# Causal attention with beacon keys and a SwiGLU FFN on one core: a scheduler-ordered kernel rewritten as one pipeline in fixed order

## The chip, the core and the metric

One core of a Trainium2 chip. TensorE (PE) multiplies, VectorE (DVE) and ScalarE (ACT) read its results from PSUM, GpSimd (POOL) works on SBUF alone, SyncE (SP) issues DMAs. PSUM has eight banks of 2 KB a partition. The metric is the device time of one execution in microseconds; lower is better.

## The reference

Eight batches, eight heads, 576 queries of 64 values. Every query sees 16 beacon keys and, causally, the 576 keys of its own batch and head. The head outputs are put side by side into 4,608 tokens of 512 values, and a gated FFN of width 1,536 follows.

```python
k_all = np.concatenate([beacon_k, k], axis=2)          # 16 + 576 keys
v_all = np.concatenate([beacon_v, v], axis=2)
scores = np.matmul(q, k_all.transpose(0, 1, 3, 2)) / np.sqrt(64)
scores = np.where(causal, -1e9, scores)                # beacons are never masked
a = np.exp(scores - scores.max(-1, keepdims=True))
a /= a.sum(-1, keepdims=True) + 1e-09
x = np.matmul(a, v_all).transpose(0, 2, 1, 3).reshape(4608, 512)
g = x @ w_gate                                         # 512 x 1536
out = (g / (1 + np.exp(-g)) * (x @ w_val)) @ w_out     # 1536 x 512
```

## The kernel before

**Inputs.** `batch_inputs` loads a batch of q, k and v with 17 DMAs from SP's queue, rows of 256 bytes (one head, one token), all heads at once into float32 staging tiles with one buffer each, and casts them to bf16 on VectorE (L102 to L110). Beacons and keys stand together in five key tiles of 128, 128, 128, 128 and 80 rows; the queries are in blocks of 128 from the first query on, the last of 64 rows. The three weights are loaded and cast by three large DMAs from GpSimd's queue, issued at the start (L119 to L123).

**Attention.** `pair_transposes` turns q and k of two heads (one head in the upper, one in the lower 64 rows) with five PE transposes each (L239, L249), and VectorE copies them out (L245, L255). `head` then goes over five key tiles: a score matmul over 64 rows, keys on the output partitions (L280, L283, L297), an Exp to bf16 on ScalarE (L285, L286, L299), on GpSimd a memset (L302) and a causal select (L287, L304). P·V (L335) takes P as the weights and V with a column of ones as the 65 moving columns, so each output has its own row sum; VectorE divides (L354 to L362) and writes to `x_all`, whose rows are tokens in blocks of 128 over all batches. As 576 is not a multiple of 128, odd batches begin half a block later, and 17 matmuls a head are needed.

**FFN.** `ffn_chunk_stages` cuts a chunk of 512 tokens into 45 pieces of work: the transposes of x (L139, L145); for each of 12 slices of the width the gate (L159) and value matmuls (L169), four each, and the elementwise step; for each of four token tiles two halves of six output matmuls (L206, L217), a copy (L224) and a DMA from GpSimd's queue (L226). The elementwise step needs Tanh and a Copy on ScalarE and two operations on VectorE:

```python
nc.scalar.activation(th[:, 0:L], g_ps[:, 0:L], ACT.Tanh, scale=0.5)   # L180
nc.scalar.activation(vv[:, 0:L], v_ps[:, 0:L], ACT.Copy, scale=0.5)   # L182
nc.vector.scalar_tensor_tensor(                                       # L184
    out=u[:, 0:L], in0=th[:, 0:L], scalar=1.0, in1=g_ps[:, 0:L],
    op0=ALU.add, op1=ALU.mult,
)
```

**Order.** Chunks whose tokens the batches before have finished go into a list; `gap()` takes one piece of it after each key tile and each query block of a head. What is left, two chunks of nine, runs after the last batch. The framework's scheduler may then move instructions on each engine by its own priorities. PSUM: four one-bank buffers for transposes, scores and outputs, three for gate and value, one for P·V.

## Time and profile before

| | |
|---|---|
| three timed runs | 545.87, 546.08 and 548.62 us, median 546.08 |
| span of the profiled execution, first to last instruction | 541.7 us |
| PE, DVE, ACT, POOL busy | 86, 49, 46 and 28% of the span |
| first PE instruction | 31.1 us |
| attention of the second batch begins | 70 us |
| granted TensorE clock, mean | 0.977 of 2.4 GHz |

The page gives busy time as the union of an engine's instructions. TensorE's matmuls overlap in the pipe, so the distance from one start to the next tells its pace, not the duration. An idle time counts only where the engine is the bottleneck. The profiled execution's time is its span and what lies around it; the runs above were timed without the profiler.

### The profile page before, as it was taken

The page shows a single profiled execution, that of the slowest core. Times are in us where ns is not written, and L with a number is a line of the kernel's source. Part 1 is how long each engine was busy: PE and PEld are TensorE (multiplying, and loading weights), DVE is VectorE, ACT ScalarE, POOL GpSimd, SP SyncE. Part 2 cuts the span into 40 slices and gives each one's busy share as a digit, 9 for nine tenths or more (in the row PEclk, how much of TensorE's full clock was granted, in tenths as well). Part 3 has the DMA queues.
Part 4 walks back from the last instruction along what each step waited for, and adds up shares of the span by engine and source line. Part 5 has one row for each costly group of instructions (what it writes and reads, how often), then busy time and mean ns, then how long its engine had stood idle before and what let it go on. Part 6 is the DMA issues. An engine that isn't in the chain of part 4 may idle for free.

```text
span 541.7 us, 9489 instructions
## 1 busy us (share of the span) xinstructions
PE 463.3 (86%) x3177; PEld 220.2 (41%) x3232; DVE 267.6 (49%) x656; ACT 249.9 (46%) x601; POOL 151.0 (28%) x629
## 2 busy tenths in 40 slices
PE   0028989988999799898999799879999998999995
PEld 0015544434454444443444344434444444444442
DVE  0033358645656446635554465545443554364552
ACT  0004536722674256624762377225752675263460
POOL 3005424323334222342324223322333232200001
PEclk9999999989999989998999799979999999999999
DMA  9999545456523630094008500010002000201102
GB/s 170 202 225 252 122 91 123 106 131 168 122 59 74 188 85 1 7 238 102 1 2 203 142 2 2 27 52 1 1 1 79 1 1 2 79 0 40 39 2 77
DMA packets 120353, 43.61 MB, mean 81 GB/s; under 512 B 115440, under 2 KB 116976, under 8 KB 120304
## 3 DMA queue, kind: packets, MB, share of 16 engines
q1 hardware_dynamic: 114816, 28.84, 24.0%
q0 software_dynamic: 5488, 14.16, 9.3%
q8 instruction: 25, 0.41, 0.3%
q14 instruction: 24, 0.20, 0.1%
HBM read 38.27 MB, written 9.44 MB: 88 GB/s over the span
## 4 chain that ended last, share of the span: by engine, by line
PE 68%; issue 15%; SPq 6%; DVE 6%; ACT 2%; POOL 2%; DMA 1%; POOLq 0%; DVEq 0%; ACTq 0%
PE g_ps L159 14%; PE v_ps L169 14%; PE s_ps L297 8%; PE o_ps L335 8%; PE o_ps L206 7%; PE o_ps L217 7%; PE s_ps0a L280 4%; SPq L74 3%; SPq L91 2%; PE xt_ps L139 2%; PE qt_ps L239 2%; PE kt_ps L249 1%; DVE kt_pair L255 1%; DVE v5p L109 1%; ACT pT L299 1%
## 5 line engine op out<-in xcount | busy, mean ns | idle before, releaser
L299 ACT ACTIVATE pT<-s_ps 128x464 bf16<-128x464 f32 (+3 forms) x256 | 91.0, 402 | 58.7 <-PE s_ps L297 55.4
L159 PE MATMUL g_ps<-xT,wg 128*128 128x512 bf16 x404 | 113.2, 388 | 3.7 <-DVE xT L145 1.8
L184 DVE SCALAR_TENSOR_TENSOR u<-th,g_ps 128x512 bf16<-128x512 bf16 x108 | 74.2, 687 | 82.5 <-ACT th L180 81.3
L169 PE MATMUL v_ps<-xT,wv 128*128 128x512 bf16 x421 | 112.9, 381 | 1.0 <-ACT vv L182 0.3
L285 ACT ACTIVATE pT<-s_ps0a 128x512 bf16<-128x512 f32 x64 | 38.2, 596 | 129.4 <-PE s_ps0b L283 125.5
L304 POOL TENSOR_SCALAR_AFFINE_SELECT pT<-pT 128x128 bf16<-128x128 bf16 (+1 forms) x256 | 72.8, 295 | 87.3 <-ACT pT L299 85.4
L180 ACT ACTIVATE th<-g_ps 128x512 bf16<-128x512 f32 x108 | 64.9, 601 | 55.9 <-PE g_ps L159 55.9
L287 POOL TENSOR_SCALAR_AFFINE_SELECT pT<-pT 128x112 bf16<-128x112 bf16 x64 | 24.8, 388 | 214.0 <-ACT pT L285 203.7
L182 ACT ACTIVATE vv<-v_ps 128x512 bf16<-128x512 f32 x108 | 64.7, 599 | 31.5 <-PE v_ps L169 31.2
L335 PEld LDWEIGHTS <-pT 128*128 128x128 bf16 (+3 forms) x1088 | 52.8, 104 | 34.6 <-issue 9.0
L297 PE MATMUL s_ps<-qt_pair,kt_pair 64*128 64x464 bf16 (+3 forms) x256 | 64.4, 304 | 1.1 <-ACT pT L285 0.6
L335 PE MATMUL o_ps<-v5p,pT 128*128 128x65 bf16 (+3 forms) x1088 | 63.1, 202 | 1.2 <-POOL pT L287 0.4
L188 DVE TENSOR_TENSOR hT<-u,vv 128x512 bf16<-128x512 bf16 x108 | 46.2, 427 | 34.4 <-ACT vv L182 34.0
L224 DVE COPY o_sb<-o_ps 128x512 f32<-128x512 f32 x36 | 24.9, 692 | 70.9 <-PE o_ps L217 70.9
L159 PEld LDWEIGHTS <-wg 128*128 128x128 bf16 x432 | 36.2, 99 | 44.7 <-issue 12.4
L169 PEld LDWEIGHTS <-wv 128*128 128x128 bf16 x432 | 36.9, 98 | 42.3 <-issue 8.0
L206 PE MATMUL o_ps<-wo,hT 128*128 128x512 bf16 x208 | 52.9, 387 | 0.2
L217 PE MATMUL o_ps<-wo,hT 128*128 128x512 bf16 x208 | 52.6, 381 | 0.5
L280 PE MATMUL s_ps0a<-qt_pair,kt_pair 64*128 64x512 bf16 x64 | 27.1, 423 | 25.1 <-DVE kt_pair L255 24.7
L239 PE MATMUL qt_ps<-ident,q4p 128*128 128x128 bf16 (+1 forms) x160 | 18.2, 227 | 33.0 <-DVE q4p L102 31.1
L297 PEld LDWEIGHTS <-kt_pair 64*128 64x128 bf16 (+1 forms) x256 | 21.2, 105 | 61.4 <-issue 55.4
L302 POOL MEMSET pT<- 128x48 bf16 (+3 forms) x256 | 39.6, 172 | 6.7 <-PE o_ps L335 6.5
(36 smaller groups left out, 310.1 us busy)
## 6 DMA issues: line engine op xcount, KB each, us to landing
out_dram<-o_sb POOLq DMA_DIRECT2D x36, 256.0 KB, 2.3
q<-in_q_dram SPq DMA_DIRECT2D x32, 256.0 KB, 3.7
k<-in_k_dram SPq DMA_DIRECT2D x24, 256.0 KB, 4.3
v<-in_v_dram SPq DMA_DIRECT2D x24, 256.0 KB, 3.9
k<-in_k_dram SPq DMA_DIRECT2D x8, 224.0 KB, 3.8
v<-in_v_dram SPq DMA_DIRECT2D x8, 224.0 KB, 3.0
wg<-in_moe_w_gate_dram POOLq DMA_DIRECT2D x1, 1536.0 KB, 13.2
wv<-in_moe_w_val_dram POOLq DMA_DIRECT2D x1, 1536.0 KB, 20.1
```

The source lines that it names most:

```text
L159: nc.tensor.matmul(g_ps[:, 0:L], lhsT=wg[:, kk, DFF_CHUNK * f : DFF_CHUNK * f + DFF_CHUNK], rhs=xT[kk][:, 0:L], start=(kk == 0), stop=(kk ...
L169: nc.tensor.matmul(v_ps[:, 0:L], lhsT=wv[:, kk, DFF_CHUNK * f : DFF_CHUNK * f + DFF_CHUNK], rhs=xT[kk][:, 0:L], start=(kk == 0), stop=(kk ...
L180: nc.scalar.activation(th[:, 0:L], g_ps[:, 0:L], ACT.Tanh, scale=0.5)
L182: nc.scalar.activation(vv[:, 0:L], v_ps[:, 0:L], ACT.Copy, scale=0.5)
L184: nc.vector.scalar_tensor_tensor(out=u[:, 0:L], in0=th[:, 0:L], scalar=1.0, in1=g_ps[:, 0:L], op0=ALU.add, op1=ALU.mult,)
L206: nc.tensor.matmul(o_ps[0:li, 0:DM], lhsT=hT[:, f, 128 * i : 128 * i + li], rhs=wo[:, f, :], start=(f == 0), stop=False,)
L217: nc.tensor.matmul(o_ps[0:li, 0:DM], lhsT=hT[:, f, 128 * i : 128 * i + li], rhs=wo[:, f, :], start=False, stop=(f == NF - 1),)
L280: nc.tensor.matmul(sa[:, :], lhsT=Kt[:, 0:P], rhs=Qt[:, 0:512], start=True, stop=True)
L297: nc.tensor.matmul(sp[0:kr, 0:ncomp], lhsT=Kt[:, 128 * t : 128 * t + kr], rhs=Qt[:, qr:S], start=True, stop=True)
L299: nc.scalar.activation(ptt[0:kr, u0 : u0 + ncomp], sp[0:kr, 0:ncomp], ACT.Exp, scale=0.125)
L304: nc.gpsimd.affine_select(out=ptt[0:kr, u0 : u0 + W], in_=ptt[0:kr, u0 : u0 + W], compare_op=ALU.is_ge, fill=0.0, base=0, pattern=[[1, W]] ...
L335: nc.tensor.matmul(oreg(ci)[0:L, :], lhsT=pT[t][0:kr, off : off + L], rhs=v5p[0:kr, t, h, 0 : D + 1], start=(idx == 0), stop=(idx == len(t ...
```

## The change

The scheduler is switched off (`manual_schedule`), so every engine runs its instructions in the order in which the program names them. The parts:

- Query blocks follow the key tiles: 112, 128, 128, 128 and 80 queries, so that block c needs key tiles 0 to c, 15 P·V matmuls a head, for every batch alike. x lives in a tile per batch; its transposes (`x_transpose`) write to one `xT` tile over all tokens, a pair of heads at a time.
- Scores come in two bursts for a pair of heads. In a burst the matmuls of the two heads alternate, one in the upper, one in the lower 64 rows. Each head's burst fills a two-bank PSUM tile and has a single Exp (976 or 720 columns), followed by two or three selects. The memsets inside the loop are gone.
- Gate and value of a slice share a two-bank tile; one Silu on ScalarE and one multiply on VectorE take the place of the four operations.
- Scores and gate/value share three two-bank buffers (`big`); transposes and P·V share one bank (`att`), the outputs have one (`outp`).
- In each batch b: attention of b, with the output halves of chunk b-1 between the bursts; then gate and value of chunk b, the first three slices begun while the last heads end; beside them the casts of batch b+1 (two on VectorE and one on GpSimd per slice) and its q and k transposes, all four pairs.
- First batch: loads, casts and transposes pair by pair; gate and value weights in four quarters, issued behind each pair's second burst; the output weights later. The load of batch b+2 is issued after the FFN of batch b, as 31 DMAs; output DMAs go from SP's queue.

```diff
+KPAD = NKT * P
+TOK = 512
+QBLOCKS = [(0, 112), (112, 128), (240, 128), (368, 128), (496, 80)]
+P1_USED, P1_W = 976, 1024
+P2_USED, P2_W = 720, 768
+SCORES1 = [(0, 0, 0, 512), (1, 512, 112, 464)]
+SCORES2 = [(0, 0, 496, 80), (2, 80, 240, 336), (4, 416, 480, 96), (3, 512, 368, 208)]
+MASKS1 = [(0, 112, NB), (512, 128, 0)]
+MASKS2 = [(80, 128, 0), (416, 96, -16), (512, 128, 0)]
...
+    sg_pool = ctx.enter_context(tc.tile_pool(name="sg", bufs=3))
     hT_pool = ctx.enter_context(tc.tile_pool(name="hT", bufs=2))
...
+    o_pool = ctx.enter_context(tc.tile_pool(name="o", bufs=3))
+    big = ctx.enter_context(tc.tile_pool(name="big", bufs=3, space=bass.MemoryType.PSUM))
+    att = ctx.enter_context(tc.tile_pool(name="att", bufs=1, space=bass.MemoryType.PSUM))
+    outp = ctx.enter_context(tc.tile_pool(name="outp", bufs=1, space=bass.MemoryType.PSUM))
+
+    ctx.enter_context(tc.manual_schedule())
...
+    def load_q(b, h0, h1):
+        d = stage["q32"]
+        for h in range(h0, h1):
             nc.sync.dma_start(
...
+                d[:, 0:4, h, :], q[b, h, 0:512, :].rearrange("(c p) d -> p c d", p=P)
             )
...
+    def load_w(i):
+        cols = slice(384 * i, 384 * i + 384)
+        for t, src in ((wg, moe_w_gate), (wv, moe_w_val)):
+            nc.gpsimd.dma_start(t[:, :, cols], src[:, cols].rearrange("(kk p) f -> p kk f", p=P))
...
+    def transpose_q(m, copy):
+        t_ps = att.tile([P, KPAD], BF16, name="t_ps", tag="att")
+        for c in range(NKT):
+            nc.tensor.transpose(t_ps[:, P * c : P * c + P], qb[:, c, 2 * m : 2 * m + 2, :], ident[:])
+        copy(qT[m][:, 0:S], t_ps[:, 0:S])
...
+    def scores(m, which, spec, used, masks):
+        s = [big.tile([P, 1024], FP32, name="s_ps", tag="big") for _ in range(2)]
+        for t, col, q0, n in spec:
+            for hh in range(2):
+                r = slice(64 * hh, 64 * hh + 64)
+                nc.tensor.matmul(
+                    s[hh][:, col : col + n],
+                    lhsT=kT[m][r, P * t : P * t + P],
+                    rhs=qT[m][r, q0 : q0 + n],
+                    start=True,
+                    stop=True,
                 )
...
+        for hh in range(2):
+            p = pt[2 * (m % 2) + hh][which]
+            nc.scalar.activation(p[:, 0:used], s[hh][:, 0:used], ACT.Exp, scale=0.125)
+            for col, n, base in masks:
+                nc.gpsimd.affine_select(
...
+    def pv(b, m, hh, x):
+        h = 2 * m + hh
+        o_ps = att.tile([P, NKT, 68], FP32, name="pv_ps", tag="att")
+        for c, (q0, _) in enumerate(QBLOCKS):
+            for t in range(c + 1):
+                w, col = p_slice(t, q0)
+                nc.tensor.matmul(
+                    o_ps[:, c, 0 : D + 1],
+                    lhsT=pt[2 * (m % 2) + hh][w][:, col : col + P],
+                    rhs=vb[b % 2][:, t, h, 0 : D + 1],
+                    start=(t == 0),
+                    stop=(t == c),
                 )
...
+        rec = rec_pool.tile([P, NKT, 1], FP32, name="rec")
+        nc.vector.reciprocal(rec[:], o_ps[:, :, D : D + 1])
         nc.vector.tensor_tensor(
...
+    def x_transpose(b, m, x):
+        t_ps = att.tile([P, S], BF16, name="xt_ps", tag="att")
+        for c, (q0, n) in enumerate(QBLOCKS):
+            nc.tensor.transpose(
+                t_ps[:, q0 : q0 + n], x[0:n, c, P * m : P * m + P], ident[0:n, 0:n]
+            )
+        nc.vector.tensor_copy(xT[:, m, S * b : S * b + S], t_ps[:])
...
+    def gv_mm(j, f, k0, k1):
+        if k0 == 0:
+            gv[f] = big.tile([P, 1024], FP32, name="gv_ps", tag="big")
...
+        for half, w in ((0, wg), (1, wv)):
+            for kk in range(k0, k1):
+                nc.tensor.matmul(
+                    gv[f][:, TOK * half : TOK * half + TOK],
...
+    def gv_act(j, f):
+        sg = sg_pool.tile([P, TOK], BF16, name="sg")
+        nc.scalar.activation(sg[:], gv[f][:, 0:TOK], ACT.Silu)
+        nc.vector.tensor_tensor(out=hTs[j][:, f, :], in0=sg[:], in1=gv[f][:, TOK:1024], op=ALU.mult)
...
+                if w == 1:
+                    o_sb = o_pool.tile([P, DM], FP32, name="o_sb")
+                    nc.vector.tensor_copy(o_sb[:], o_ps[:])
+                    r = TOK * j + P * i
+                    nc.sync.dma_start(out[r : r + P, :], o_sb[:])
...
+    def prep_first(m):
+        h0, h1 = 2 * m, 2 * m + 2
+        for f in cast_pieces(kb, "k32", h0, h1, 80, nc.vector):
+            f()
+        transpose_k(m, dve_copy)
+        for f in cast_pieces(qb, "q32", h0, h1, 64, nc.vector):
+            f()
+        transpose_q(m, dve_copy)
+        for f in cast_pieces(vb[0], "v32", h0, h1, 80, nc.gpsimd):
+            f()
+
+    prep_first(0)
+    fillers = []
...
     for b in range(B):
...
+        x = x_pool.tile([P, NKT, DM], BF16, name="x")
+        for m in range(NPAIR):
+            scores1(m)
+            if m:
+                pv(b, m - 1, 0, x)
+            fill()
+            scores2(m)
+            if b == 0:
+                load_w(m)
+                if m + 1 < NPAIR:
+                    prep_first(m + 1)
+            if m:
+                pv(b, m - 1, 1, x)
+            fill()
+            if m:
+                x_transpose(b, m - 1, x)
+        j = b
+        last = NPAIR - 1
+        gv_mm(j, 0, 0, KD - 1)
+        pv(b, last, 0, x)
+        gv_mm(j, 1, 0, KD - 1)
+        pv(b, last, 1, x)
+        gv_mm(j, 2, 0, KD - 1)
+        x_transpose(b, last, x)
+        if b == 0:
+            load_batch(1)
+            for i in range(2):
+                load_wo(i)
+        casts, trans, vcasts = [], [], []
         if b + 1 < B:
...
+            vcasts = cast_pieces(vb[(b + 1) % 2], "v32", 0, H, 80, nc.gpsimd)
+            casts = cast_pieces(kb, "k32", 0, H, 80, nc.vector) + cast_pieces(
+                qb, "q32", 0, H, 64, nc.vector
+            )
+            for m in range(NPAIR):
+                trans.append(lambda m=m: transpose_k(m, dve_copy))
+                trans.append(lambda m=m: transpose_q(m, act_copy))
+        f_cast = 0 if b else 7
+        for f in range(NF):
+            if f < 3:
+                gv_mm(j, f, KD - 1, KD)
+            else:
+                gv_mm(j, f, 0, KD)
+            gv_act(j, f)
+            if f >= f_cast:
+                for _ in range(2):
+                    if casts:
+                        casts.pop(0)()
+                if vcasts:
+                    vcasts.pop(0)()
+            if not casts and trans and f >= 4:
+                trans.pop(0)()
+        while trans:
+            trans.pop(0)()
+        if b + 2 < B:
+            load_batch(b + 2)
+        fillers = out_halves(j)
+    j = NCH - 1
+    for f in range(NF):
+        gv_mm(j, f, 0, KD)
+        gv_act(j, f)
+        fill()
+    while fillers:
+        fill()
+    for half in out_halves(j):
+        half()
```

## Rows read from the trace of the kernel before

**Rows 1.** The page, part 1: busy us, share of the span, instructions.

```profile
PE 463.3 (86%) x3177; PEld 220.2 (41%) x3232; DVE 267.6 (49%) x656; ACT 249.9 (46%) x601; POOL 151.0 (28%) x629
```

**Rows 2.** Stages: length; busy us of each engine; granted clock; DMA share; GB/s.

```profile
0.00:31.10 31.10, 0.00 (x0) 0.00 (x0) 1.23 (x1) 1.28 (x1) 4.29 (x15) 1.00 1.05 187
...
70.00:127.00 57.00, 51.18 (x332) 23.00 (x339) 35.16 (x82) 28.39 (x69) 17.17 (x70) 0.97 0.54 125
...
415.00:472.00 57.00, 53.81 (x401) 25.39 (x408) 29.16 (x78) 29.83 (x74) 16.33 (x75) 1.00 0.06 21
472.00:541.70 69.70, 63.09 (x298) 28.67 (x301) 34.38 (x64) 28.33 (x48) 4.32 (x8) 0.99 0.09 34
```

**Rows 3.** Timeline, TensorE, 478 us to the end: start, us, what.

```profile
478.96 1.03 PE L159 MATMUL g_ps<-xT,wg 128*128 128x512 bf16 x4
479.82 1.03 PE L169 MATMUL v_ps<-xT,wv 128*128 128x512 bf16 x4
...
503.13 1.33 PE L139 MATMUL xt_ps<-ident,x_all 128*128 128x128 bf16 x16
...
534.46 1.46 PE L217 MATMUL o_ps<-wo,hT 128*128 128x512 bf16 x6
```

**Rows 4.** Timeline, all engines, about 441 us: P·V weights and transposes.

```profile
441.22 0.67 PEld L335 LDWEIGHTS <-pT 128*128 128x128 bf16 x14
...
441.86 0.52 PE L239 MATMUL qt_ps<-ident,q4p 128*128 128x128 bf16 x5
...
442.31 0.43 PE L249 MATMUL kt_ps<-ident,k5p 128*128 128x128 bf16 x5
```

**Rows 5.** The same timeline, TensorE among output matmuls, 456 to 460 us.

```profile
456.19 1.47 PE L206 MATMUL o_ps<-wo,hT 128*128 128x512 bf16 x6
...
457.60 0.31 PE L297 MATMUL s_ps<-qt_pair,kt_pair 64*128 64x336 bf16 x1
...
457.84 1.47 PE L217 MATMUL o_ps<-wo,hT 128*128 128x512 bf16 x6
...
459.24 0.26 PE L297 MATMUL s_ps<-qt_pair,kt_pair 64*128 64x208 bf16 x1
...
459.43 1.47 PE L206 MATMUL o_ps<-wo,hT 128*128 128x512 bf16 x5
```

**Rows 6.** Waits: us in total, times, longest us.

```profile
PE s_ps0a L280 <- DVE kt_pair L255: 24.7, 16, 3.2
```

**Rows 7.** Groups by shape: busy us, mean ns; idle before.

```profile
L180 ACT ACTIVATE th<-g_ps 128x512 bf16<-128x512 f32 x108 | 64.9, 601 | 55.9 <-PE g_ps L159 55.9
...
L285 ACT ACTIVATE pT<-s_ps0a 128x512 bf16<-128x512 f32 x64 | 38.2, 596 | 129.4 <-PE s_ps0b L283 125.5 <-PE o_ps L335 3.8
...
L286 ACT ACTIVATE pT<-s_ps0b 128x64 bf16<-128x64 f32 x64 | 14.1, 220 | 0.0
L285 ACT ACT_TABLE_LOAD x1 | 1.3, 1283 | 0.8 <-PEq L422 0.8
...
L184 DVE SCALAR_TENSOR_TENSOR u<-th,g_ps 128x512 bf16<-128x512 bf16 x108 | 74.2, 687 | 82.5 <-ACT th L180 81.3
...
L255 DVE COPY kt_pair<-kt_ps 128x592 bf16<-128x592 bf16 x32 | 14.6, 455 | 1.3 <-PE kt_ps L249 1.1
...
L106 DVE CAST k5p<-k 80x512 bf16<-80x512 f32 x8 | 3.8, 481 | 0.0
...
L304 POOL TENSOR_SCALAR_AFFINE_SELECT pT<-pT 128x128 bf16<-128x128 bf16 x192 | 58.0, 304 | 85.1 <-ACT pT L299 83.9
```

**Rows 8.** Timeline, SP's queue, the first batch's loads: start, us.

```profile
33.74 0.85 SPq L96 DMA_DIRECT2D k<-in_k_dram  x1
...
35.20 0.43 SPq L85 DMA_DIRECT2D v<-in_v_dram  x1
```

**Rows 9.** The page, part 3: DMA queues, share of 16 engines' span.

```profile
q1 hardware_dynamic: 114816, 28.84, 24.0%
q0 software_dynamic: 5488, 14.16, 9.3%
```

More of the change, by code (lines that the diff above doesn't have):

```diff
@@ L68 @@
-    po = ctx.enter_context(tc.tile_pool(name="po", bufs=1, space=bass.MemoryType.PSUM))
-    def batch_inputs(b):
-        q32 = stage_pool.tile([P, QC, H, D], FP32, name="q32")
-        for c in range(QC):
-            L = min(128, S - 128 * c)
+    KD = DM // P
+    NF = DFF // P
+    NCH = NTOK // TOK
+    NPAIR = H // 2
+    assert NCH == B + 1
+    static = ctx.enter_context(tc.tile_pool(name="static", bufs=1))
+    x_pool = ctx.enter_context(tc.tile_pool(name="x", bufs=2))
+    rec_pool = ctx.enter_context(tc.tile_pool(name="rec", bufs=3))
@@ new lines @@
+    ident = static.tile([P, P], BF16, name="ident")
+    stage = {n: static.tile([P, NKT, H, D], FP32, name=n) for n in ("q32", "k32", "v32")}
+    qb = static.tile([P, NKT, H, D], BF16, name="qb")
+    kb = static.tile([P, NKT, H, D], BF16, name="kb")
+    vb = [static.tile([P, NKT, H, 68], BF16, name=f"vb{i}") for i in range(2)]
+    qT = [static.tile([P, KPAD], BF16, name=f"qT{m}") for m in range(NPAIR)]
+    kT = [static.tile([P, KPAD], BF16, name=f"kT{m}") for m in range(NPAIR)]
+    pt = [
+        (static.tile([P, P1_W], BF16, name=f"p1_{i}"), static.tile([P, P2_W], BF16, name=f"p2_{i}"))
+        for i in range(4)
+    ]
@@ new lines, in load_kv, with load_batch, cast_pieces, main @@
+                d[:, 1:4, h, :], src[b, h, 112:496, :].rearrange("(c p) d -> p c d", p=P)
+            )
+        nc.sync.dma_start(
+            d[0:80, 4, h0:h1, :], src[b, h0:h1, 496:S, :].rearrange("h p d -> p h d")
+        )
+    def load_batch(b):
+        load_kv("k32", k, beacon_k, b, 0, H)
+        load_q(b, 0, H)
+        load_kv("v32", v, beacon_v, b, 0, H)
+    def cast_pieces(dst, name, h0, h1, last, engine):
+        src = stage[name]
+        def main(c0, c1):
+            engine.tensor_copy(dst[:, c0:c1, h0:h1, 0:D], src[:, c0:c1, h0:h1, :])
+        def tail():
+            engine.tensor_copy(dst[0:last, 4, h0:h1, 0:D], src[0:last, 4, h0:h1, :])
+        if h1 - h0 == H:
+            return [lambda c=c: main(c, c + 1) for c in range(4)] + [tail]
+        return [lambda: main(0, 4), tail]
@@ new lines, in transpose_k, with dve_copy, act_copy @@
+    def transpose_k(m, copy):
+        t_ps = att.tile([P, KPAD], BF16, name="t_ps", tag="att")
+        for c in range(NKT):
+            L = P if c < 4 else 80
+            nc.tensor.transpose(
+                t_ps[:, P * c : P * c + L], kb[0:L, c, 2 * m : 2 * m + 2, :], ident[0:L, 0:L]
+            )
+        copy(kT[m][:, 0 : NB + S], t_ps[:, 0 : NB + S])
+    def dve_copy(o, i):
+        nc.vector.tensor_copy(o, i)
+    def act_copy(o, i):
+        nc.scalar.activation(o, i, ACT.Copy)
+    def scores(m, which, spec, used, masks):
[9 more added lines that the diff above has]
+                    stop=True,
+                )
+        for hh in range(2):
[3 more added lines that the diff above has]
+                nc.gpsimd.affine_select(
+                    out=p[:, col : col + n],
+                    in_=p[:, col : col + n],
+                    compare_op=ALU.is_ge,
+                    fill=0.0,
+                    base=base,
+                    pattern=[[1, n]],
+                    channel_multiplier=-1,
+                )
@@ new lines, in gv_act, with out_halves, half @@
+    def gv_act(j, f):
+        sg = sg_pool.tile([P, TOK], BF16, name="sg")
+        nc.scalar.activation(sg[:], gv[f][:, 0:TOK], ACT.Silu)
+        nc.vector.tensor_tensor(out=hTs[j][:, f, :], in0=sg[:], in1=gv[f][:, TOK:1024], op=ALU.mult)
+    def out_halves(j):
+        halves = []
+        for i in range(TOK // P):
+            st = {}
+            def half(w, i=i, st=st):
+                if w == 0:
+                    st["o"] = outp.tile([P, DM], FP32, name="o_ps", tag="outp")
+                o_ps = st["o"]
+                for f in range(6 * w, 6 * w + 6):
+                    nc.tensor.matmul(
+                        o_ps[:],
+                        lhsT=hTs[j][:, f, P * i : P * i + P],
+                        rhs=wo[:, f, :],
+                        start=(f == 0),
+                        stop=(f == NF - 1),
+                    )
+                if w == 1:
[3 more added lines that the diff above has]
+                    nc.sync.dma_start(out[r : r + P, :], o_sb[:])
+            halves += [lambda half=half: half(0), lambda half=half: half(1)]
+        return halves
```

375 lines of the change are left out of this document (60 added, 315 removed).

## The prediction

> **What bounds the kernel now.** I read the busy shares first [rows 1]: TensorE is busy for 463 of 541.7 us, every other engine for half of the span or less. A busy PE says little by itself, since matmuls overlap, so the next view is busy time by stage, with the stages cut where a batch's attention begins [rows 2]. The reader is to see three parts. Until 31.1 us PE does nothing, while the DMA engines are saturated. From 70 to 472 us seven batches pass in 402 us, 57.4 us each, PE busy for nine tenths of it, the others for half. The last 69.7 us hold FFN work alone.
>
> Is 57.4 us PE's own work? In the FFN tail a group of four 512-column matmuls starts every 0.865 us, so 0.216 us each [rows 3]. A chunk has 96 of them for gate and value and 48 for the output: 31.1 us. A batch's eight heads have 8 x 1,664 score columns, at the same pace per column 5.6 us. The weight loads of P·V, 14 in 0.67 us of which the last takes 0.10, go by at 0.044 us each [rows 4]; 136 of them are 6.0 us. Q/K transposes take 0.09 us each (five from 441.86 to 442.31), x transposes 0.08 (16 in 1.33) [rows 3, 4]: 40 and 16 of them are 4.9 us. Together 47.6. What is left, 9.8 us a batch, has two sources in the rows. Between 456.19 and 459.43 stand twelve 512-column matmuls and two scores (336 and 208 columns), whose columns need 2.82 of 3.24 us: 0.42 us goes to four changes between 128-row and 64-row matmuls, 0.105 us each [rows 5]. And the scores wait for the copy of K^T, 24.7 us in all, some 3 us a batch [rows 6]. So TensorE bounds every batch, and each batch pays about 10 us that is not columns.
>
> **The change, PE's work in one batch.** FFN: the same 31.1 us. Scores: per head 976 + 720 = 1,696 columns, eight heads 13,568 columns. If the alternating heads run one after the other, 5.7 us; if they run at once, 2.9. Nowhere in this trace do matmuls on different array halves stand side by side, so neither end is shown. I take 2.9: the shapes (64*128) show each score using half of the rows, the two heads use opposite halves, and their outputs go to different banks. P·V: 15 instead of 17 per head, 120 x 0.044 = 5.3. Transposes: 40 x 0.09 + 20 x 0.08 = 5.2. Changes of row mode: two bursts a pair, eight a batch, two changes each, 16 x 0.105 = 1.7; the 64-row Q transposes, which changed the mode too, are padded to 128 rows. Sum 46.2 us.
>
> The Trainium skill (TensorE: Matmul & The Clock Gate, "Part 3: Packing small matmuls") says that matmuls on different row groups run concurrently, and gives 3.07x for four. That agrees with 2.9; no row here shows it, and without it a batch's sum is 49.0.
>
> **Waits that the fixed order adds, per batch.** Scores and gate/value share three two-bank buffers.
> FFN to attention: call 0 the end of the last gate/value pair. ScalarE still owes Silu (0.60, the Tanh row) and the last Q^T copy (0.65, the Exp line at 576 columns), then, if Silu needs another table than Exp, a load of 1.28 us, then an Exp over 976 columns: from 596 ns at 512 columns and 220 at 64, 0.839 ns a column, so 0.98 [rows 7]. First Exp done at 3.7. PE covers 0.4 (transposes), 0.5 (first burst), 1.3 (an output half), 2.2 in all; its second burst needs the first Exp's buffer: 1.5 us of wait, and 0.5 later on the masks of the first pair. I take 2.0; with no load 0.7; with a change of twice the load 3.3.
> Attention to FFN: the table load falls in some 4 us without ScalarE work and costs nothing; without that cover 1.28. But the three gate/value groups held open for the last quarter of x wait for its copy (0.46 and the semaphores, 0.7), and the fourth group waits for Silu 0.60 and the multiply 0.69 less what PE does meanwhile, 0.7.
> One shared P·V/transpose bank: 0.2 us on three pairs, 0.6. Sum of waits 4.0, so a batch takes 50.2 us.
>
> **Do other engines fit?** ScalarE per batch: sixteen Exps (0.98 and 0.77) 14.0, twelve Silu 7.2, four copies 2.6, two loads 2.6: 26.4 of 50. VectorE: twelve multiplies at the 687 ns of the scalar_tensor_tensor from PSUM, 8.3; P·V scaling, eight times no more than 0.7, 5.6; eight copies at 0.46 and four at some 0.69, 6.4; ten casts at 0.48, 4.8: 25. GpSimd: per head five selects at 0.304, so 12; five V casts, no row of that kind, bounded by VectorE's 0.48 and the select's pace per column, 1.2 us: 2 to 6; the 32 memsets a batch are gone. The removed Copy and half of the VectorE work thus gain nothing by themselves. The tight place is the FFN stretch: two casts and a multiply are 1.65 us of VectorE against 1.73 of PE per step.
> SP: a batch load grows from 17 to 31 issues at 0.43 to 0.85 us [rows 8], 13 to 26 us, and the output writes now queue behind it. It can begin when the casts are done, some 9 us into the FFN stretch, and is due at the next, 41 us later: hidden, and so are the writes, with three buffers.
>
> **Start.** The first load no longer competes with the weights. A pair has 13 DMAs at about 0.45 us: first pair landed near 9 us. Four pairs: 24 us of issue. DMA time: inputs 24.0% of the span over 8 batches, 16.3 us each. q0 has 9.3%, 50 us; the end stage moved its nine last output tiles in 6.3 us of DMA time, so 36 tiles 25 us, and the weights 25, gate and value 17 [rows 2, 9]. Three quarters of these come before the last pair: 29 us, so the last pair lands at 28 to 34, I take 31. Its chain of casts, transposes and copies takes 3, its two bursts and P·V 4: FFN from 38. Gate/value 20.7, P·V and x 1.8, waits 1.4: 62. Here the casts wait for the second batch (f from 7 on), so seven transposes with their copies come alone, 1.06 us each: the second batch's attention begins at 69 us (62 if they hide, 78 if the second load is late), against 70, but with a chunk's gate and value done.
>
> **Sum.** 69 + 7 x 50.2 - 3.6 (no next batch at the last) = 416.8. Then the last chunk's gate/value 20.7 and the previous one's eight output halves 10.4; the last output 10.4, plus 0.9 us at each of three tiles for the copy out of its one bank (0.69 and the semaphores): 2.7. The end stays: last PE work until 535.9, span end 541.7, 5.8 us [rows 3]. 50.0 in all. Span 466.8. The median of the runs, 546.1, is 4.4 us over the profiled span; with these 471 us.
>
> **Rivals.**
> *The bursts don't overlap.* 2.8 us a batch on seven: 491. For it: all score rows are paced by their columns; against it: these are all of one half.
> *Casts and buffers bind in the FFN stretch.* If a cast takes 0.72 instead of 0.48 while GpSimd casts V beside it, a step has 2.13 us of VectorE against 1.73 of PE: 0.40 on five steps, 2.0 a batch, and as much again where the copies of the next batch queue behind: 485 to 499, 495 as its time. For it: the margin of 0.08, and that no row has both engines casting; against it: the margin is paid back in the seven steps without casts.
> *A table change costs twice its load.* 1.28 more on seven transitions: 480. For it: the order has Silu straight before Exp each time; against it: the only load of the trace is 1.28.
> The skill (ScalarE: Activation LUTs, "What ACT_TABLE_LOAD costs") gives 1,283 ns, as this trace does, and a drain of 1,380 beside it, by which the sum would be 481; no row here shows the drain.
> *Slower than before.* The casts stand between the multiplies on VectorE, in fixed order. If a batch's inputs land late, the cast blocks the multiply, the multiply the buffer, the buffer PE. To lose the 75 us gained it must cost 10.7 us in each of seven batches, on top of the 15 us of slack that a load has (41 against 26): a load of over 50 us. Against it: a batch needs 16.3 us of DMA time, and the DMA share of a batch is 0.54 at first and 0.06 at last [rows 2]. Time, from that point on, 550.
>
> **Numbers.** Forecast 471, chance 0.60, its own range 452 to 486. No overlap 0.15, casts 0.11, table 0.08, slower 0.05; 0.01 for a change of under 0.5%, about what a measurement of this kernel can tell from no change. The range starts at 452 (no table loads, 9 us; start at 62, 7 us; and a little of the waits) and reaches to 502, past the first two rivals, which leaves out one in ten below and above each. Faster by over 0.5%: 0.94; within 0.5%: 0.01; slower: 0.05.
>
> **What would show it.** First transpose at about 9 us; the FFN of the first batch from 38; from one batch's first burst to the next 50 us. In a burst, the starts of the two heads' matmuls a few tens of ns apart (right) or 0.2 us (wrong). Sixteen table loads of 1.28 us, and a PE wait of 1.5 us in the second burst after each FFN stretch. VectorE under 1.73 us per FFN step. Wrong would be: PE waiting in the FFN stretch for VectorE, SP issuing a load into the next FFN stretch, or a start that reaches beyond 80 us.

## The result: 458.2 us against 546.0

Four runs of the changed kernel have a median of 458.19 us (457.54 to 458.49), those of the kernel before 545.98: a ratio of 0.839 [0.8353, 0.8427]. The forecast was 471 with 452 to 502. The time is inside its range and 12.8 us under the forecast, and that distance is a sum of terms of both signs, which the rows show one by one.

The span is 456.8 us. The page of the kernel after, part 1 [rows 1]:

```profile
PE 391.2 (86%) x3068; PEld 199.8 (44%) x3120; DVE 196.8 (43%) x439; ACT 204.0 (45%) x280; POOL 113.2 (25%) x383
```

PE has the same busy share as before, of a span that is 85 us shorter: 72 us of its busy time are gone. By stages (length; busy us of each engine; granted clock; DMA share; GB/s) [rows 2]:

```profile
0.00:42.80 42.80, 20.45 (x193) 12.68 (x194) 14.51 (x51) 14.98 (x18) 20.18 (x64) 1.00 0.89 155
...
125.50:172.90 47.40, 43.09 (x368) 22.22 (x373) 22.52 (x51) 24.84 (x34) 12.81 (x45) 1.00 0.45 99
...
408.24:456.80 48.56, 41.88 (x189) 18.66 (x191) 14.38 (x21) 7.76 (x13) 0.00 (x0) 0.99 0.12 44
```

A steady batch takes 47.4 us (from first burst to first burst, too: 174.08 to 221.50) where the forecast had 50.2 and the kernel before 57.4. The second batch's attention begins at 78.08 us (forecast 69), the last part from 408.24 on takes 48.6 us (forecast 50.0).

One steady batch in the timeline of TensorE (start, us, what; in brackets idle time before and what ended it) [rows 3 to 5]:

```profile
176.00 0.21 PE L176 MATMUL s_ps<-qT,kT 64*128 64x80 bf16 x1
177.40 0.47 PE L176 MATMUL s_ps<-qT,kT 64*128 64x80 bf16 x7 [1.19 <-ACT p L185]
177.80 1.47 PE L267 MATMUL o_ps<-wo,hT 128*128 128x512 bf16 x6
179.20 0.58 PE L176 MATMUL s_ps<-qT,kT 64*128 64x512 bf16 x4
179.72 0.63 PE L209 MATMUL pv_ps<-vb,p 128*128 128x65 bf16 x15
180.18 1.46 PE L267 MATMUL o_ps<-wo,hT 128*128 128x512 bf16 x6
181.57 0.48 PE L176 MATMUL s_ps<-qT,kT 64*128 64x80 bf16 x8
181.99 0.62 PE L209 MATMUL pv_ps<-vb,p 128*128 128x65 bf16 x15
...
185.05 0.62 PE L209 MATMUL pv_ps<-vb,p 128*128 128x65 bf16 x15 [0.37 <-DVE xT L231]
...
195.70 0.38 PE L244 MATMUL gv_ps<-xT,wg 128*128 128x512 bf16 x1 [0.45 <-DVE xT L231]
...
203.03 1.02 PE L244 MATMUL gv_ps<-xT,wg 128*128 128x512 bf16 x4 [0.54 <-DVE hT L255]
...
206.48 0.42 PE L160 MATMUL t_ps<-ident,kb 128*128 128x128 bf16 x5
206.74 1.03 PE L244 MATMUL gv_ps<-xT,wg 128*128 128x512 bf16 x4
...
209.14 0.44 PE L153 MATMUL t_ps<-ident,qb 128*128 128x128 bf16 x5 [0.51 <-DVE kT L166]
```

Read the distances between starts, not the durations. A first burst, 1,952 columns in four matmuls, takes 0.52 us (179.20 to 179.72); at the pace of [rows 3], 0.216 us for 512 columns, it would be 0.82. Fifteen P·V take 0.46, five transposes 0.26. An idle time in brackets is shorter than the delay, because a matmul's modelled end reaches past the next start: the second burst of the first pair, 176.00 to 177.80, costs 1.38 us more than the 0.42 of its like at 181.57, and 1.19 of it shows as a wait.

ScalarE in the same batch, and the groups by shape over the whole span [rows 7]:

```profile
175.07 1.28 ACT L185 ACT_TABLE_LOAD   x1
...
194.27 1.28 ACT L254 ACT_TABLE_LOAD   x1
201.66 1.58 ACT L254 ACTIVATE sg<-gv_ps 128x512 bf16<-128x512 f32 x3 [6.11 <-PE gv_ps L244]
```

```profile
L185 ACT ACTIVATE p<-s_ps 128x976 bf16<-128x976 f32 x64 | 59.5, 981 | 47.0 <-PE s_ps L176 43.7 <-POOL p L187 1.9 <-PE pv_ps L209 1.3
...
L185 ACT ACT_TABLE_LOAD x8 | 10.3, 1283 | 1.2 <-PEq L400 0.8 <-PE s_ps L176 0.3
L254 ACT ACT_TABLE_LOAD x8 | 10.3, 1283 | 0.1
```

The load for Exp stands on the path (from 175.07 to 176.36; the burst goes on at 177.40, as the first Exp of 0.98 is done); the load for Silu is over 6 us before a Silu is due.

The start, TensorE with the queues of GpSimd and SP [rows 8]:

```profile
5.42 0.67 PE L160 MATMUL t_ps<-ident,kb 128*128 128x128 bf16 x5 [5.42 <-DVE kb L129]
...
16.10 1.00 PE L209 MATMUL pv_ps<-vb,p 128*128 128x65 bf16 x15
17.04 0.95 PE L176 MATMUL s_ps<-qT,kT 64*128 64x80 bf16 x8
...
43.78 17.33 SPq L101 DMA_DIRECT2D q<-in_q_dram  x8
...
67.67 0.42 PE L160 MATMUL t_ps<-ident,kb 128*128 128x128 bf16 x5
70.28 0.44 PE L153 MATMUL t_ps<-ident,qb 128*128 128x128 bf16 x5 [2.19 <-DVE kT L166]
```

The second batch's q takes 17.33 us for eight issues, beside the last quarter of the gate and value weights and the output weights (42.91 to 46.06 on GpSimd's queue); the third batch's goes out at seven issues in 3.77 us from 76.47 on. All eight groups of transposes then stand alone between 67.67 and 78.08.

### The profile page after: what moved, and what is told of

The parts are those of the page before. It is cut to its first block, busy times and chain, and to the rows that moved or that the text cites. A ratio compares the mean times of both kernels' runs of the same rounds, so it can differ in the third digit from the quotient of the medians.

```text
span 456.8 us, 8189 instructions
## 1 busy us (share of the span) xinstructions
PE 391.2 (86%) x3068; PEld 199.8 (44%) x3120; DVE 196.8 (43%) x439; ACT 204.0 (45%) x280; POOL 113.2 (25%) x383
## 4 chain that ended last, share of the span: by engine, by line
PE 68%; DVE 16%; ACT 6%; SPq 3%; DMA 3%; issue 3%; DVEq 0%; ACTq 0%
PE gv_ps L244 32%; PE o_ps L267 19%; PE pv_ps L209 8%; PE s_ps L176 4%; DVE o_sb L276 4%; DVE hT L255 4%; DMA v<-in_v_dram 3%; DVE xT L231 3%; ACT sg L254 2%; PE t_ps L153 2%; DVE qb L129 2%; ACT L185 2%; PE t_ps L160 1%; DVE kb L129 1%; ACT p L185 1%
## 5 line engine op out<-in xcount | busy, mean ns | idle before, releaser
L187 POOL TENSOR_SCALAR_AFFINE_SELECT p<-p 128x112 bf16<-128x112 bf16 (+2 forms) x320 | 80.3, 285 | 227.3 <-ACT p L185 225.9
L254 ACT ACTIVATE sg<-gv_ps 128x512 bf16<-128x512 f32 x108 | 62.8, 597 | 162.9 <-PE gv_ps L244 155.6
L185 ACT ACTIVATE p<-s_ps 128x720 bf16<-128x720 f32 (+1 forms) x128 | 104.5, 876 | 61.9 <-PE s_ps L176 56.7
L244 PE MATMUL gv_ps<-xT,wg 128*128 128x512 bf16 x414 | 113.8, 380 | 13.1 <-DVE xT L231 7.8
L244 PE MATMUL gv_ps<-xT,wv 128*128 128x512 bf16 x426 | 114.3, 381 | 0.3
L255 DVE TENSOR_TENSOR hT<-sg,gv_ps 128x512 bf16<-128x512 bf16 x108 | 73.6, 685 | 93.1 <-ACT sg L254 93.1
L267 PEld LDWEIGHTS <-hT 128*128 128x128 bf16 x432 | 38.5, 98 | 46.0 <-issue 8.6
L209 PEld LDWEIGHTS <-p 128*128 128x128 bf16 x960 | 37.4, 101 | 24.1 <-issue 9.2
L276 DVE COPY o_sb<-o_ps 128x512 f32<-128x512 f32 x36 | 24.9, 691 | 53.4 <-PE o_ps L267 53.4
L209 PE MATMUL pv_ps<-vb,p 128*128 128x65 bf16 x960 | 42.3, 199 | 6.3 <-DVE xT L231 5.2
L176 PE MATMUL s_ps<-qT,kT 64*128 64x336 bf16 (+5 forms) x384 | 39.5, 307 | 9.3 <-ACT p L185 8.1
```

What stands on the lines that cost most here:

```text
L176: nc.tensor.matmul(s[hh][:, col : col + n], lhsT=kT[m][r, P * t : P * t + P], rhs=qT[m][r, q0 : q0 + n], start=True, stop=True,)
L185: nc.scalar.activation(p[:, 0:used], s[hh][:, 0:used], ACT.Exp, scale=0.125)
L187: nc.gpsimd.affine_select(out=p[:, col : col + n], in_=p[:, col : col + n], compare_op=ALU.is_ge, fill=0.0, base=base, pattern=[[1, n]], c ...
L209: nc.tensor.matmul(o_ps[:, c, 0 : D + 1], lhsT=pt[2 * (m % 2) + hh][w][:, col : col + P], rhs=vb[b % 2][:, t, h, 0 : D + 1], start=(t == 0 ...
L244: nc.tensor.matmul(gv[f][:, TOK * half : TOK * half + TOK], lhsT=w[:, kk, P * f : P * f + P], rhs=xT[:, kk, TOK * j : TOK * j + TOK], star ...
L254: nc.scalar.activation(sg[:], gv[f][:, 0:TOK], ACT.Silu)
```

## The experiments

Each is the kernel after with one edit, except where said. Times are medians; each group had its own runs of the kernel before (544.35, 546.0 and 543.85 us), so kernels of different groups are compared by their ratios; differences in us are those of the medians, and by the ratios they come out up to 2 us otherwise. A second check is the steady batch in the profile, from one first burst to the next. The kernel after has 0.839 [0.8353, 0.8427].

### Do the two heads' bursts run at once?

**Both heads on the upper 64 rows** (the second head's scores come from the first head's q and k).

```diff
-                r = slice(64 * hh, 64 * hh + 64)
+                r = slice(0, 64)
```

> The changed kernel with both heads of a burst computed on the upper 64 rows (the second head's scores are made from the first head's q and k, so its part of the output is another one); all else stays. Since heads in turn ran as fast as alternating ones, the overlap must come from the two halves and not from the order. Theory: without it a first burst needs 0.82 us of columns instead of 0.41 and a second 0.61 instead of 0.30, 0.7 us a pair, 20 us in seven batches, of which 2 may hide behind the wait in the first pair; 476 to 478. Rival (bursts are short for another reason): 458.

472.18 us, ratio 0.8681 [0.8642, 0.872]: 14.0 us slower than after.

```profile
183.58 0.74 PE L176 MATMUL s_ps<-qT,kT 64*128 64x80 bf16 x7 [0.78 <-ACT p L185]
...
185.66 0.99 PE L176 MATMUL s_ps<-qT,kT 64*128 64x512 bf16 x4
186.59 0.63 PE L209 MATMUL pv_ps<-vb,p 128*128 128x65 bf16 x15
```

The bursts of a pair now take 0.93 and 0.73 us instead of 0.52 and 0.42: 0.72 a pair, 2.9 a batch, what the prediction gave for no overlap. The batch grows by 1.6 only (47.4 to 49.0), since the longer burst covers waits: the bank wait before P·V is gone, and the first pair waits 0.78 for the Exp instead of 1.19. So without the overlap a batch loses little more than half of the 2.8 us that the rival had. Another 2.65 of the 14.0 us stand ahead of the second batch's attention (80.73 instead of 78.08).

**The heads in turn**, first head's matmuls and then the second's, still on opposite halves.

```diff
-            for t, col, q0, n in spec:
-                for hh in range(2):
+            for hh in range(2):
+                for t, col, q0, n in spec:
```

> The changed kernel with the two heads of a burst one after the other instead of alternating; nothing else. Theory (matmuls on opposite halves of the array run at once, which is why a burst of 1,952 columns takes 0.52 us in the profile): each pair gets about 0.7 us longer on TensorE, in seven batches of four pairs about 20 us, less some 0.3 us in the first pair of a batch where a wait for ScalarE stands anyway; 475 to 478 us. Rival (a burst is short for another reason, such as the clock or fewer columns): 458, no change.

458.43 us, 0.8415 [0.8388, 0.8442]: no difference. My theory, that the alternation makes the overlap, fell.

```profile
177.84 0.39 PE L176 MATMUL s_ps<-qT,kT 64*128 64x512 bf16 x2
...
178.36 0.63 PE L209 MATMUL pv_ps<-vb,p 128*128 128x65 bf16 x15
```

The program's order is 512, 464 columns for one head, then 512, 464 for the other. Yet within 0.01 us of 177.84 two matmuls of 512 columns have started, and P·V follows after 0.52 us, as in the alternating order. So, as the starts have it, each half of the rows takes up its own next matmul. What the overlap needs is the opposite half, not the order.

**Bursts cut**: one output matmul after each key tile but the last, so twelve changes of row mode a pair instead of four.

```diff
@@ scores
+            if t != spec[-1][0]:
+                one()
...
@@ out_halves
-            halves += [lambda half=half: half(0), lambda half=half: half(1)]
+            halves += [lambda mm=mm, f=f: mm(f) for f in range(NF)]
```

> The changed kernel with one output matmul put after each key tile of a burst but the last (taken from the output half that follows): the same matmuls, the two heads still alternate, but a pair has twelve changes of row mode instead of four. Theory (a change costs 0.105 us, as read between output and score matmuls of the kernel before): 8 x 0.105 us a pair, four pairs, seven batches, 23 us, less what the first pair hides; 476 to 482. Rival (a change costs nothing that overlap does not hide): 458.

483.52 us, 0.886 [0.8828, 0.8891]: 25.3 us more for 8 x 4 x 7 = 224 changes, 0.113 us each. The steady batch says the same: 51.05 us instead of 47.42, 0.113 for each of 32 changes. This agrees with the 0.105 of [rows 5]. Grouping the scores in two bursts a pair saves 3.6 us a batch against this cut, the overlap 1.6.

### What does the table change cost, and where?

**Tanh in place of Silu**, which needs no other table than Exp.

```diff
-        nc.scalar.activation(sg[:], gv[f][:, 0:TOK], ACT.Silu)
+        nc.scalar.activation(sg[:], gv[f][:, 0:TOK], ACT.Tanh)
```

> The changed kernel with Tanh in place of Silu, so that the FFN's output is another function's; the shapes and the engines are the same, and Tanh and Exp shared one table load in the kernel before. Theory (a load of 1.28 us is on the path once per batch, where the FFN ends, and hidden where it begins): one load instead of sixteen, minus 1.2 us in each of seven batches, about 450 us. Rival one (all hidden): 458. Rival two (every change costs a drain as well, as the Trainium skill's page ScalarE: Activation LUTs has it, 2.66 us): about 440.

449.73 us, 0.8258 [0.8234, 0.8282]: 8.5 us less (7.2 by the ratios), 1.0 to 1.2 for each of seven batches. In the profile a steady batch takes 46.04 us instead of 47.42, 1.38 less.

```profile
172.30 1.47 PE L267 MATMUL o_ps<-wo,hT 128*128 128x512 bf16 x6
173.70 0.48 PE L176 MATMUL s_ps<-qT,kT 64*128 64x80 bf16 x8
```

The second burst follows the output half without a wait. One load a batch is on the path, at about its own 1,283 ns. The Trainium skill (ScalarE: Activation LUTs, "What ACT_TABLE_LOAD costs") adds a drain of 1,380 ns to each load; by an estimate from its two figures seven changes less on the path would have given 18.6 us, and this run, with 8.5, doesn't show the drain.

**Both output halves before the second burst** of the first pair, so that PE has work while the table loads.

```diff
             scores1(m)
...
             fill()
+            if m == 0:
+                fill()
             scores2(m)
...
-            fill()
+            if m:
+                fill()
```

> The changed kernel, but in the first pair of each batch both output halves stand before the second burst, so that TensorE has 1.3 us more work while ScalarE loads its table. Theory (the limit there is ScalarE's chain of a load and four Exps, and the three buffers that they empty): the wait of 1.2 us leaves the second burst and comes back at the first burst of the second pair, 458 plus or minus 2. Rival (the wait is only a matter of what TensorE has to do in that place): minus 1.2 us in seven batches, 450.

458.3 us, 0.8404 [0.8376, 0.8432]: no difference in time.

```profile
179.23 0.56 PE L176 MATMUL s_ps<-qT,kT 64*128 64x80 bf16 x8
180.20 0.37 PE L176 MATMUL s_ps<-qT,kT 64*128 64x512 bf16 x1 [0.41 <-ACT p L185]
180.86 0.57 PE L176 MATMUL s_ps<-qT,kT 64*128 64x512 bf16 x3 [0.29 <-ACT p L185]
```

The wait moved to the next pair's first burst, which follows at once and needs a buffer that ScalarE has not read yet: P·V follows at 181.36, 1.19 us later than without a wait. The late chain is ScalarE's; work put ahead of one burst is work missing ahead of the next. What is left, 0.23 us a steady batch (47.19), the profiled run lost again at the start, where its second batch's attention began at 79.46 instead of 78.08.

**Three output halves in the first pair**, 3-2-2-1 instead of 2-2-2-2.

```diff
+            if m == 0:
+                fill()
...
-            fill()
+            if m < NPAIR - 1:
+                fill()
```

> The changed kernel with the eight output halves spread 3, 2, 2, 1 over the four pairs instead of 2, 2, 2, 2, the third one of the first pair also before the second burst. Theory (as for the run with both halves first, but now the chain on ScalarE has 1.3 us more of TensorE work beside it, and the last pair still has 4.0 us of TensorE against 3.5 of ScalarE): minus 0.9 to 1.2 us in seven batches, 450 to 452. Rival (the last pair becomes bound by ScalarE and gives it back): 458.

452.81 us, 0.8312 [0.8286, 0.8338]: 5.4 us less (4.3 by the ratios); a steady batch takes 46.43 us, 0.99 less, since the first pair has one half more of cover. What is left there is the single output bank: the third half waits for the copy (0.43 us by starts).

```profile
177.72 1.45 PE L267 MATMUL o_ps<-wo,hT 128*128 128x512 bf16 x6 [0.28 <-DVE o_sb L276]
```

**Silu in the kernel before**: its four elementwise operations replaced by Silu and one multiply, and nothing else.

```diff
-                nc.scalar.activation(th[:, 0:L], g_ps[:, 0:L], ACT.Tanh, scale=0.5)
-                nc.scalar.activation(vv[:, 0:L], v_ps[:, 0:L], ACT.Copy, scale=0.5)
-                nc.vector.scalar_tensor_tensor(
...
+                nc.scalar.activation(sg[:, 0:L], g_ps[:, 0:L], ACT.Silu)
...
-                    out=hT[:, f, 0:L], in0=u[:, 0:L], in1=vv[:, 0:L], op=ALU.mult
+                    out=hT[:, f, 0:L], in0=sg[:, 0:L], in1=v_ps[:, 0:L], op=ALU.mult
```

> The kernel before with one Silu and one multiply in place of Tanh, Copy and two VectorE operations; its order stays. Theory (the shorter elementwise step gains nothing where TensorE is the bound, and Silu pays only in an order that keeps it apart from Exp): 84 of the 108 Silus stand among Exps, up to two table loads of 1.28 us each, up to 215 us more on ScalarE, a good part of it in the way of TensorE; 560 to 640. Rival (fewer operations help, the loads hide): 535 to 546.

630.36 us against 543.85 there, a ratio of 1.1582 [1.1532, 1.1632].

```profile
L180 ACT ACT_TABLE_LOAD x85 | 109.1, 1283 | 1.5
```

84 more and the first stand at the Exps: 170 loads in all against one, in the kernel after 16. In the old order Silu costs 86.5 us; it needs an order that keeps FFN and attention apart on ScalarE. Whether it beats the four operations in the new order was not tried.

### What holds up the second batch?

**Casts from the fourth FFN step on** instead of the eighth, in the first batch.

```diff
-        f_cast = 0 if b else 7
+        f_cast = 0 if b else 3
```

> The changed kernel, but the casts of the second batch stand from the fourth step of the first FFN stretch on instead of the eighth. They then wait for q, whose loads compete with the weights until about 62 us. Theory (a cast that waits for a DMA blocks the multiplies behind it, these the buffers, these TensorE): a TensorE wait of 4 to 8 us in the first FFN stretch, which eats most of the 5 to 6 us that transposes beside the matmuls save; 456 to 460. Rival (casts early are simply better): 452.

462.23 us, 0.8459 [0.8418, 0.8499]: 4.0 us more. VectorE and TensorE, and then two windows (length, busy us of each engine, granted clock, DMA share, GB/s):

```profile
65.28 0.43 DVE L129 CAST qb<-q 128x512 bf16<-128x512 f32 x1 [8.14 <-DMA v<-in_beacon_v_dram]
...
68.67 0.69 PE L153 MATMUL t_ps<-ident,qb 128*128 128x128 bf16 x5 [7.77 <-DVE kT L166]
69.15 1.91 PE L244 MATMUL gv_ps<-xT,wg 128*128 128x512 bf16 x4
70.86 1.91 PE L244 MATMUL gv_ps<-xT,wv 128*128 128x512 bf16 x4
```

```profile
64.00:68.60 4.60, 0.00 (x0) 0.10 (x1) 3.31 (x9) 0.00 (x0) 0.61 (x1) 0.53 0.91 201
68.67:73.06 4.39, 4.39 (x18) 2.15 (x18) 0.54 (x1) 0.91 (x2) 2.28 (x4) 0.50 0.91 202
```

The cast of q waits 8.14 us for its load (the releaser is inferred; the load of q ends just ahead of the one named), multiplies and copies wait behind the cast, PE behind these. This is the mechanism of the rival "slower than before", in one batch. PE idles 7.77 us, and the granted clock falls to 0.50, 1.2 GHz: four 512-column matmuls take 1.71 us instead of 0.865.

**The same, with the output weights issued only in the eighth and ninth steps** (f of 7 and 8).

```diff
-            for i in range(2):
-                load_wo(i)
...
-        f_cast = 0 if b else 7
+        f_cast = 0 if b else 3
...
+            if b == 0 and f in (7, 8):
+                load_wo(f - 7)
```

> As the run with early casts, and the output weights are loaded from the eighth step of the first FFN stretch on, behind the second batch's q. Theory (the start is set by what the DMA engines carry ahead of q): q lands about 8 us earlier, the casts wait little, four or five of the seven lone transposes find cover; 450 to 453. Rival (the output weights are then late for the first output halves): 458 or more.

455.56 us, 0.8334 [0.8294, 0.8375]: 2.6 us less, short of what was expected. The second batch's attention begins 5.3 us earlier, at 72.80, but (issues of SP and of GpSimd, then TensorE):

```profile
46.17 9.09 SPq L101 DMA_DIRECT2D q<-in_q_dram  x8
...
65.17 0.82 POOL L145 DMA_DIRECT2D wo<-in_moe_w_out_dram  x1
...
79.56 2.72 PE L267 MATMUL o_ps<-wo,hT 128*128 128x512 bf16 x6 [1.80 <-DMA wo<-in_moe_w_out_dram]
```

The issue stood on GpSimd's queue behind casts of V that waited for their load, so the weights came too late for the output, and the second batch takes 51.79 us instead of 48.59. The output weights had indeed slowed q, by enough to block the casts: without them eight issues of q take 9.09 us instead of 17.33, and the cast of q waits 0.46 instead of 8.14.

### Is the fixed order itself worth anything?

**The scheduler left on.**

```diff
-    ctx.enter_context(tc.manual_schedule())
```

> The changed kernel without the line that keeps the program's order, so that the framework's scheduler may move instructions again. Theory (the gain needs the order: Exps and Silus kept apart, bursts kept whole): more table loads than sixteen and more changes of row mode, 470 to 520 us. Rival (the parts gain by themselves, the order nothing): 458.

453.25 us, 0.8304 [0.8259, 0.8348]: 4.9 us less. My theory, that the scheduler mixes Silu and Exp, fell: there are 16 table loads here too.

```profile
131.89 0.48 PE L175 MATMUL s_ps<-qT,kT 64*128 64x80 bf16 x4
132.30 0.82 PE L266 MATMUL o_ps<-wo,hT 128*128 128x512 bf16 x3
133.28 0.47 PE L175 MATMUL s_ps<-qT,kT 64*128 64x80 bf16 x4 [0.16 <-ACT p L184]
```

It keeps the program's order in the large and puts output matmuls into the wait for the first Exp. A batch takes 45.9 us (131.0 to 176.9) instead of 47.4; the second batch's attention begins later, at 82 us instead of 78. The gain of the change lies in how its work is cut and laid out, not in the fixed order, which costs 4.9 us here.

### The corrections together

Halves 3-2-1-1, the last one behind the x transposes of the last pair; casts from the fourth step; the output weights behind q, held back on GpSimd by reading a result of the fifth step; the last output in the three two-bank buffers.

```diff
-                    st["o"] = outp.tile([P, DM], FP32, name="o_ps", tag="outp")
+                    if tail:
+                        st["o"] = big.tile([P, 1024], FP32, name="o_tail", tag="big")[:, 0:DM]
...
-            fill()
+            if m < 2:
+                fill()
...
         x_transpose(b, last, x)
+        fill()
...
+            if b == 0 and f == 4:
+                nc.gpsimd.tensor_copy(gate[:], hTs[0][:, 4, 0:8])
+                for i in range(2):
+                    load_wo(i)
```

> The changed kernel with what the runs pointed to, in fixed order: output halves 3, 2, 1, 1 over the pairs and one more behind the last x transposes, where TensorE waits 0.55 us for their copy; casts of the second batch from the fourth step; the output weights loaded behind q of the second batch (GpSimd first reads a result of the fifth step) and ahead of the V casts; the last output in the three large buffers instead of one bank. Theory (the waits are in different places and add up): 5.4 by the halves, 3 to 4 behind the x transposes, 6 to 8 at the start, 2.3 at the end; 438 to 443. Rival (the pairs with one half are now bound by ScalarE, or the output weights are late): 448 to 455.

446.61 us, 0.8196 [0.8166, 0.8227], the best of all: 11.6 us under the kernel after (10.6 by the ratios).

```profile
181.00 0.43 PE L229 MATMUL xt_ps<-ident,x 112*128 112x112 bf16 x5 [0.82 <-DVE x L219]
...
428.04 10.52 PE L271 MATMUL o_tail<-wo,hT 128*128 128x512 bf16 x47
```

The second batch begins 6.3 us earlier, a batch takes 46.7 us, the last output runs without the three waits. The rest of the expected gain went into a new wait: in pairs with one half, x's transposes wait for VectorE (17 times and 13.9 us in all, against 3 times and 2.4 us in the kernel after).

**The same with the scheduler on.**

> The same as the run with all the changes, without the line that keeps the program's order. Theory (the scheduler takes the program's order as priorities and fills the waits that the halves were moved for; only start and end still gain): the scheduler's 453 less 2.3 at the end and 3 to 6 at the start, 444 to 448. Rival (order and scheduler add up): 436 to 440.

447.66 us, 0.8227 [0.8203, 0.8251]: not to be told from the fixed order. Its batches are shorter (45.6 us, 130.0 to 175.6), its second batch begins at 82 us instead of 71.75. An order that has both was not tried.

## Why the prediction was right, and what offset what

**The start, mis-sized by 9.1 us (69 against 78.08).** The first transpose came at 5.42 us, not 9. But the attention of the first batch ran at half pace: fifteen P·V took 0.94 us (16.10 to 17.04) against 0.46 later. From the last pair's first transposes at 32.20 to the FFN at 42.80 it was 10.6 us where the prediction had 7 from a landing at 31: FFN from 42.8 instead of 38, +4.8. By an estimate from the starts of the nine groups of matmuls in these 10.6 us, the half pace is about 3.5 of them. The kernel before ran its first batch at that pace, too (nineteen P·V from 58.08 to 59.38, 0.068 us each), so its trace could have shown it; the prediction priced the start with rows from 441 us.

The first chunk took 24.9 us instead of 24, +0.9. And eight groups of transposes alone took 10.4 us instead of the 7 (seven groups of 1.06) that the forecast had, +3.4: the first K copy stood behind the casts of q (2.19 us), and from 73.61 on the clock was at 0.50.

That 78 was also the upper bound given for the start is luck: its reason, "the second load is late", did not come into play, as no cast on VectorE waits for a load between 42.8 and 78.08. The casts stand in the eighth step by the program. What the load's lateness does is to make earlier casts useless, as the runs with early casts show, and the output weights are part of it.

**Score bursts and mode changes, exact.** 2.9 + 1.7 us were predicted. Measured: 4 x (0.52 + 0.42) with the change behind each burst, and 0.10 for the one ahead of it (177.80 to 179.20 is 1.40 for six matmuls of 0.216): 4.6. One rule of the Trainium skill (TensorE: Matmul & The Clock Gate, "Part 3: Packing small matmuls") was weighed there, that matmuls on different row groups run concurrently; 1,952 columns in 0.52 us, a change of row mode with them, agree, and on one half they take 0.93.

**P·V, 0.044 against 0.031.** The prediction took the pace of the weight loads of [rows 4]. The matmuls of that very group stood in the same trace, and by their starts (441.44 to the transposes at 441.86) fourteen took 0.42 us, 0.030 each:

```profile
441.44 0.58 PE L335 MATMUL o_ps<-v5p,pT 128*128 128x65 bf16 x14
```

In the kernel after fifteen take 0.46 us: 120 are 3.7 us, 1.6 less. 65 columns at 0.216/512 are 0.027, so the pace is near that of the columns; whether these or the weight loads set it, the runs don't separate.

**Transposes, 0.09 and 0.08 against 0.054.** Five take 0.26 to 0.28 us; twelve groups a batch are 3.2 us, 2.0 less. Again it is near the columns' pace (128 x 0.216/512 = 0.054). Of the 0.08, the duration of a merged group in [rows 3] holds the end of the pipe. The 0.09 was read from starts, but the fifth transpose of that group is of 64 rows, so the 0.45 us hold two changes of row mode (4 x 0.054 + 0.027 + 2 x 0.105 = 0.45), which the prediction had just padded away.

**Waits, 4.0 against some 4.9.** By distances of starts: second burst 1.38 (1.5 predicted, though the four terms of its "first Exp done at 3.7" add up to 3.5), begin of the FFN 0.62, 0.71 and 0.70 (1.4), shared bank twice 0.43 (0.6), and one that was not foreseen, a Q transpose that waits 0.67 for the K copy to leave the bank (209.14); the 0.5 on the masks did not come. PE's work, 46.2 less the 1.6 and 2.0 above, is 42.6; with these waits it makes 47.5 us, the batch that was measured.

**Seven batches.** 330.2 us (78.08 to 408.24) against 7 x 50.2 - 3.6 = 347.8: -17.6.

**The last part.** 48.6 against 50.0: -1.4. The three waits for the copy are as predicted:

```profile
446.39 2.75 PE L267 MATMUL o_ps<-wo,hT 128*128 128x512 bf16 x12 [0.78 <-DVE o_sb L276]
```

The next tile starts at 449.92, 3.53 us on, and twelve matmuls at 0.216 are 2.59, so a wait is 0.94 (0.9 predicted). What is shorter is the end: the last matmul ends at 452.67, 4.1 us before the span does, where the prediction kept the 5.8 of the kernel before, whose last write went out from GpSimd's queue and not from SP's.

**What lies outside the span.** I took 4.4 us, the median of the runs less the span of another execution. The profiled execution took 458.49 us with its span of 456.8: 1.7, and so it was in every run of the experiments. -2.7.

The sum: 471 + 9.1 - 17.6 - 1.4 - 2.7 = 458.4. The mechanisms of the batch were right (bursts that overlap, one table load on the path, casts that don't bind); several sizes were not, and that the errors of the start and of the batches have opposite signs is luck: with the start as forecast, the time would have been some 449, under the range's lower end.

**The rivals.** Bursts that don't overlap: false, by the run on one half. Table change at twice its load: false, by the Tanh run; one load a batch on the path, as in the forecast. Casts that bind the FFN stretch: false in this trace as a wait for buffers. A cast takes 0.42 us, two with a multiply are 1.44 of 1.73 us, and PE's list of waits names no cast after the start. But the rival's condition was not met, and that is luck: GpSimd's five casts of V (612 ns each) run from 195.07 to 197.90, ahead of VectorE's (202.89 to 208.71). Where the two meet, the rival's price is even low: in the run with the heads in turn a cast of VectorE at 68.19, beside one of GpSimd at 68.09, takes 0.83 us. The second half of that rival, copies that queue behind casts, is there in small: it is the 0.67 us above. The K transposes begin at 206.48, and their copy only at 208.64, as VectorE is still at casts of q. Slower than before: the mechanism is real and cost some 8 us of PE's time in one batch when the casts were moved ahead; in the steady batches no such wait is in TensorE's list.

## What to carry to other kernels

When small matmuls stand close together, price them by their columns, and read the pace from the distance of starts in a dense stretch; a weight load's or a merged group's duration is no pace. Group the 64-row matmuls and put the two heads on opposite halves: the overlap saved 14 us here, and the grouping 25 against a cut behind every key tile. Price the first batch by rows of a first batch. After a reordering, look for the load whose consumer stands in fixed order among critical work, and keep ScalarE functions of different tables in different stretches.

## What the runs showed of the hardware that I had not expected

- Matmuls of the two row halves start side by side even when the program puts all of one head first: two of 512 columns within 0.01 us of 177.84, ahead of a 464-column one that stands between them in the program. The time is the same (458.43 against 458.19 us).
- A cast of VectorE that begins while GpSimd casts takes 0.83 us instead of 0.41 (68.19 with the heads in turn, 67.72 with Tanh, 66.16 and 68.26 with the scheduler); one that began 0.05 us ahead of GpSimd's (67.92 with the scheduler) took 0.42.
- The clock fell in a stretch of lone transposes. In the kernel after PE is busy 1.72 of the 5.94 us before 73.61; from there to 80.50 the granted clock is 0.50, 1.2 GHz:

```profile
67.67:73.61 5.94, 1.72 (x21) 1.28 (x20) 2.65 (x7) 1.90 (x3) 2.28 (x4) 0.98 0.92 203
73.61:80.50 6.89, 4.81 (x27) 2.71 (x28) 0.93 (x2) 2.64 (x4) 0.00 (x0) 0.50 0.78 167
```

- At the start the record says 1.00 (0 to 42.8 us) while matmuls go by at half pace: two of 512 columns start 0.43 us apart at 43.65. The trace's first entry of the clock begins at 46.0 us only, and there the pace doubles (fifteen P·V 0.77 us from 45.35 on, 0.46 from 47.41 on). Before it the 1.00 stands for no entry, and the pace is the better witness.
